# Making weights earlier and summing units later in a fused attention and two-layer feed-forward kernel

## The chip, the cores and the metric

The kernel runs on one core of a Trainium2 chip. Its time is device microseconds of one execution. The engines are TensorE (PE, with its weight loads as PEld), VectorE (DVE), ScalarE (ACT), GpSimd (POOL) and SyncE (SP), which here issues every DMA. Each takes its instructions in the order of its own list.

## The reference

```python
scores = scale * np.matmul(q, k.transpose(0, 1, 3, 2))        # 4 batches, 12 heads, 448 tokens, 64
scores = np.einsum('bhij,hg->bgij', scores, w_pre)
attn = np.exp(scores - np.max(scores, axis=-1, keepdims=True))
attn = attn / (np.sum(attn, axis=-1, keepdims=True) + 1e-09)
attn = np.einsum('bhij,hg->bgij', attn, w_post)
x = np.matmul(attn, v)                                        # as [1792, 768]
h = x @ w_in                                                  # layer 0: w_in [768, 2048]
x = (h * np.cos(h)) @ w_out                                   #          w_out [2048, 768]
g, val = x @ w_gate, x @ w_val                                # layer 1: [768, 1536] each
out = (g * (1.0 / (1.0 + np.exp(-g))) * val) @ w_out2         #          [1536, 768]
```

## The kernel before

Attention comes first. Its 180 blocks are numbered, and each small function (`qk`, `premix`, `post`, `pv_out` and so on) is entered in a plan at the number of a block plus a lag; within one number the tuple `order` sets which kind is issued first. The output of batch b goes by DMA (`pv_out`, L300) to a tile `xs[b]` in memory, and the feed-forward reads it back as token block t = b. `early_plan` enters the first feed-forward work in the same plan, counted from `s`, the first block of the last chunk: the first two column slices of `w_in`, token blocks 0 and 1, and the first layer-0 products of both blocks.

The feed-forward keeps everything as two parts, high and low. A product is three matmuls: high x high, high x low, low x high. The weights come as 64-bit words. A half slab (`w_dma`, 384 KB, a ring of 8 raw buffers) is turned into 32-bit values by `w_shift` on ScalarE and `w_bits`, three VectorE operations (tile `f`), and `w_split` puts the high part on ScalarE and the low part on GpSimd. Slabs of the first product (`i`: w_in, w_gate, w_val) also need their largest absolute value: `w_max` takes it from each half, `w_sum` folds it, `w_sum_all` spreads it over the partitions with a tiny matmul (tile `su`), and `w_unit` makes the scale from that. `w_by` multiplies a slab's scale with the tokens' scale, one number for each token block.

`steps` runs over i. The list `seq` holds (layer, group, token block): 8 groups of 256 columns in layer 0, 6 in layer 1, four blocks each. Step i issues the first product of seq[i] (`l1`, tile `ph`, for both halves e of the group, with `hidden` behind each) and then the second product of seq[i - 1] (`l2`, tile `py`, six pieces m of three banks, each added into `acc`). In layer 0 `hidden` is k, r, Sin, r and the split into `gh` (ScalarE) and `gl` (GpSimd); in layer 1 it is Silu and one product.

The weight work stands in one list, `todo`, that `w_steps` makes: per group 4 pieces for the maxima, 12 for w_out of the group before, 12 for the group's own slabs. `fill(n)` issues up to n pieces where it is called between the matmuls; a piece has a `room`, the step from which it may be issued, and the pieces go strictly in order. `need` issues pieces until a named slab is there. `sum_up`, behind both halves of `l1`, issues `w_sum_all` and `w_unit` of the maxima that are complete.

Between the layers, `next_unit` reduces the six maxima of a finished block of `acc` (tile `mx`), spreads them with a matmul (tile `sx`) and makes the tokens' scale; `next_x` makes the new tokens, two ScalarE operations and one on GpSimd for each of six pieces. `t_new` is the block for which that is due in step i.

Of the kernel before, what the change touches and what calls it, by code (L numbers as in the profile page):

```python
# [7 lines left out]
F32 = mybir.dt.float32  # L8
# [11 lines left out]
B, H, S, D = 4, 12, 448, 64  # L20
# [9 lines left out]
RAWS = 8  # L30
# [7 lines left out]
def attention(ctx, tc, qT, kT, vN, mix, xs, ff):  # L38
# [268 lines left out]
    plan = {}  # L307
# [55 lines left out]
    for i, fn, *a in ff.early_plan(first[B - 1, 3]):  # L363
        at(i, fn, *a)

    order = ("at_hi","l1_part","post","spread","dma_v","w_sum","w_sum_all","w_unit","w_bits","hidden","den","rowmax","rec","norm_hi","dma_k","x_dma","w_dma","new_scale","pv_out","at_lo","norm_lo","lo_k","dma_q","max_v","w_max","w_shift","lo_q","split_v","x_lo","premix","scale_v","w_split","expo","x_hi","qk","hi_k","hi_q","pv")


    with tc.manual_schedule():
# [51 lines left out]
class FeedForward:  # L421


    def __init__(self, ctx, tc, xs, w_in, w_out, w_gate, w_val, w_out2, outT):
        self.ctx, self.tc, self.xs, self.outT = ctx, tc, xs, outT
        self.X, self.raw, self.part, self.G, self.W, self.PH = {}, {}, {}, {}, {}, {}
        self.n_ps = self.n_wi = 0
        self.p_x = self.pool("m_x", 2)
        self.p_const = self.pool("m_const", 1)
        self.ones = self.p_const.tile([128, 128], BF16, name="ones16")  # L430
        self.p_unit = self.pool("m_unit", 4)

        self.unit = [self.p_const.tile([128, 4], F32, name=f"unit{layer}") for layer in range(2)]
        self.scale, self.by = {}, {}
        cols = [w.rearrange("(k p) n -> p k n", p=128) for w in (w_in, w_gate, w_val)]
        rows = [w.rearrange("(f p) (m n) -> f p m n", p=128, n=128) for w in (w_out, w_out2)]
        self.win = [[cols[0]], cols[1:]]
        self.wout = rows
# [88 lines left out]
    def w_shift(self, key, z):  # L527


        nc = self.tc.nc  # L530
        top = self.raw[key, z].bitcast(F32).rearrange("p m (n w) -> p m n w", w=2)[:, :, :, 1]
        t = self.p_wr.tile([128, 3, 128], F32, tag="f", bufs=2, name="f_" + self.nm(key, z))
        by = self.one(key, 4) if key[1] == "i" else 2.0 ** -112
        nc.scalar.activation(t, top, AF.Copy, scale=by)
        self.part[key, z] = t
# [21 lines left out]
    def w_split(self, key, z):  # L557
        nc = self.tc.nc
        first = key[1] == "i"
        tag = self.slab(key)[1]  # L560
        if z == 0:
            pool = self.p_wo if not first else self.p_wi[int(self.n_wi % WI > 1)]
            self.n_wi += first
            self.W[key] = tuple(
                pool.tile([128, 6, 128], F16 if first else F32R, tag=tag + p, name=p + "_" + self.nm(key, z))
                for p in "hl"
            )
            if first and (key[0] == 0 or key[3] > 1):
                self.w_by(key)
        hi, lo = (w[:, 3 * z:3 * z + 3] for w in self.W[key])  # L570
        t = self.part.pop((key, z))
        nc.scalar.copy(hi, t)  # L572
        nc.gpsimd.tensor_tensor(lo, t, hi if first else f(hi), op=ALU.subtract)  # L573
# [25 lines left out]
    def w_steps(self):  # L599


        halves = lambda keys: [(key, z) for key in keys for z in range(2)]
        groups = [(L, g) for L in range(2) for g in range((FF1, FF2)[L] // 256)]
        outs = lambda L, g: [((L, "o", 2 * g + e), z) for z in range(2) for e in range(2)]
        seq = [("conv", outs(0, 0), 0, ("o", 0, 0))]
        for n in range(1, len(groups) + 1):
            for bi, batch in enumerate(self.batches(*groups[n]) if n < len(groups) else [()]):
                room = 4 * (n - 1)
                if batch:
                    seq.append(("max", batch, room, None))  # L610
                if bi == 0 and n > 1:
                    seq.append(("conv", outs(*groups[n - 1]), 4 * (n - 2) + 1, ("o", *groups[n - 1])))
                if batch:
                    seq.append(("conv", halves(batch), room, ("i", *groups[n], bi)))
        self.to_load = []
        out = []
        for kind, what, room, name in seq:
            if kind == "max":
                hs = halves(what)
                for j, (key, z) in enumerate(hs):  # L620
                    out.append((room, None, [
                        *([(self.new_scale, what)] if j == 0 else []), (self.w_max, key, z),
                        *([(self.w_sum, what), (self.sums.append, what)] if j == 3 else []),
                    ]))
                continue
            self.to_load += what
            for j, (key, z) in enumerate(what):
                nxt = what[j + 1] if j + 1 < len(what) else None
                for k in range(3):
                    do = [(self.w_shift, key, z)] if j == k == 0 else []  # L630
                    do.append((self.w_bits, key, z, (k,)))
                    if k == 1 and nxt:
                        do.append((self.w_shift, *nxt))
                    if k == 2:
                        do += [(self.w_split, key, z), (self.load_next,)]
                    out.append((room, name if nxt is None and k == 2 else None, do, key))
        return out
# [76 lines left out]
    def hidden(self, layer, g, t, e, fill=0):  # L714
# [8 lines left out]
        if layer == 0:  # L723
            ps = self.PH[e, 0]
            by, turn = (self.by[0, "i", 0, 2 * g + e][:, i, t:t + 1] for i in range(2))
            k = self.p_t.tile([128, S], I32, tag="t", name=f"k_{g}_{t}_{e}")
            nc.vector.tensor_scalar(k, ps, turn, 0.25, op0=ALU.mult, op1=ALU.add)
            nc.vector.scalar_tensor_tensor(r, ps, turn, k, op0=ALU.mult, op1=ALU.subtract)
            nc.scalar.activation(r, r, AF.Sin, bias=self.hpi, scale=TWOPI)
            self.fill(fill)  # L730
            nc.vector.scalar_tensor_tensor(r, ps, by, r, op0=ALU.mult, op1=ALU.mult)  # L731
        else:
            if g == 0:
                for col in range(2):
                    self.w_by((1, "i", col, e), t)
            by = [self.by[1, "i", col, 2 * g + e][:, 0, t:t + 1] for col in range(2)]
            nc.scalar.activation(r, self.PH[e, 0], AF.Silu, scale=by[0])
            nc.vector.scalar_tensor_tensor(r, self.PH[e, 1], by[1], r, op0=ALU.mult, op1=ALU.mult)  # L738
# [46 lines left out]
    def next_x(self, t, m):  # L785
        nc = self.tc.nc
        hi, lo = (x[:, m] for x in self.X[t])
        x = self.p_t.tile([128, S], F32, tag="nx", bufs=2, name=f"nx_{t}_{m}")
        nc.scalar.activation(x, self.acc[t][:, m], AF.Copy, scale=self.mx[t][:, 7:8])
        nc.scalar.copy(hi, x)  # L790
        nc.gpsimd.tensor_tensor(lo, x, hi, op=ALU.subtract)

    def early_plan(self, s):

        plan = []
        wi = (0, 0, 0, 0), (3, 4, 6, 8)
        x = ((0, 0, 0, 3, 4, 5), (1, 2, 3, 5, 6, 7)), ((6, 7, 8, 9, 10, 11), (8, 9, 10, 11, 12, 13))
        l1 = (6, 7, 7, 9, 9, 9, 9, 11, 11, 12, 12, 12), (14, 15, 16, 16, 16, 16, 17, 17, 17, 17, 20, 22)
# [25 lines left out]

    def steps(self):
        seq = [(L, g, t) for L in range(2) for g in range((FF1, FF2)[L] // 256) for t in range(4)]
        self.sums, self.done, self.mx = [], set(), {}
        self.todo = self.w_steps()
        for _ in range(RAWS):
            self.load_next()  # L830
        done = seq.index((0, 7, 0))
        for t in (2, 3):
            for m in range(6):
                self.x_dma(t, m)
                self.x_hi(t, m)
                self.x_lo(t, m)
                if t == 2:
                    self.now = 0
                    self.fill(2)
        for i in range(1, len(seq) + 1):  # L840
            self.now = i
            t_new = i - done - 2
            if i > 1 and i < len(seq):
# [4 lines left out]
                for e in range(2):  # L848
                    self.l1(L, g, t, e)
                    self.hidden(L, g, t, e, 1)  # L850
                    if e == 0:
                        if 0 <= t_new < 4:
                            self.next_unit(t_new)
                            for m in range(6):
                                self.next_x(t_new, m)
                        self.fill((1, 5)[L])
                self.sum_up()
            L, g, t = seq[i - 1]
            if t == 0:
                self.need(("o", L, g))  # L860
            for m in range(6):
                self.l2(L, g, t, m)
                if m in (1, 3):
                    self.fill(1)
            del self.G[g, t]
# [72 lines left out]
```

## Time and profile before

| | us |
|---|---|
| median of 3 runs | 1581.67 |
| lowest and highest run | 1570.64, 1582.27 |
| the profiled execution | 1579.19 |
| its span, first to last instruction | 1577.4 |
| TensorE busy in it | 1443.9 |
| mean granted TensorE clock | 0.969 |

The profiled execution's own time is 1.8 us above its span and 2.5 us under the median. Attention takes about the first 530 us, layer 0 goes to about 1050, layer 1 to the end. A busy TensorE is not TensorE at its full clock: the granted clock is given as a share of 2.4 GHz.

### The profile page before, as it was taken

The page shows a single profiled execution, that of the slowest core. Times are in us where ns is not written, and L with a number is a line of the kernel's source. Part 1 is how long each engine was busy: PE and PEld are TensorE (multiplying, and loading weights), DVE is VectorE, ACT ScalarE, POOL GpSimd, SP SyncE. Part 2 cuts the span into 40 slices and gives each one's busy share as a digit, 9 for nine tenths or more (in the row PEclk, how much of TensorE's full clock was granted, in tenths as well). Part 3 has the DMA queues.
Part 4 walks back from the last instruction along what each step waited for, and adds up shares of the span by engine and source line. Part 5 has one row for each costly group of instructions (what it writes and reads, how often), then busy time and mean ns, then how long its engine had stood idle before and what let it go on. Part 6 is the DMA issues. An engine that isn't in the chain of part 4 may idle for free.

```text
span 1577.4 us, 27033 instructions
## 1 busy us (share of the span) xinstructions
PE 1443.9 (92%) x10330; PEld 952.4 (60%) x10330; DVE 1067.9 (68%) x2251; ACT 674.2 (43%) x1422; POOL 647.9 (41%) x555
## 2 busy tenths in 40 slices
PE   4899999899997599999999999767999999999999
PEld 2466566565554366666666666445666666666666
DVE  3888888888888557777777787766345656555623
ACT  3677776776765444232232232544342222222210
POOL 1777776776757423232232232434222222222300
PEclk9899999999998799999999999879999999999999
DMA  5454454455453312121121121112121111112002
GB/s 173 127 151 146 142 153 142 141 147 154 140 169 118 117 41 60 32 69 51 36 75 40 41 70 40 51 50 62 49 61 52 53 57 55 47 59 61 1 35 105
DMA packets 93569, 133.06 MB, mean 84 GB/s; under 512 B 18848, under 2 KB 80768, under 8 KB 93440
## 3 DMA queue, kind: packets, MB, share of 16 engines
q1 hardware_dynamic: 93440, 131.34, 28.2%
q8 instruction: 81, 1.33, 0.3%
q14 instruction: 48, 0.39, 0.1%
HBM read 81.59 MB, written 11.01 MB: 59 GB/s over the span
## 4 chain that ended last, share of the span: by engine, by line
PE 68%; DVE 13%; DMA 6%; ACT 6%; issue 3%; POOL 2%; SPq 0%; ACTq 0%; DVEq 0%; POOLq 0%
PE ph L710 10%; PE ph L711 10%; PE ph L712 10%; PE py L755 7%; PE py L757 7%; PE py L756 7%; PE psm L208 6%; DMA x<-s 4%; PE pss L192 3%; PE psv L290 3%; PE psa L257 2%; PE psa L258 1%; PE psa L259 1%; DVE sm L213 1%; DVE r L731 1%
## 5 line engine op out<-in xcount | busy, mean ns | idle before, releaser
L712 PE MATMUL ph<-x,l_i 128*128 128x448 f16 x960 | 340.9, 355 | 4.2 <-POOL l_i L573 4.2
L710 PE MATMUL ph<-x,h_i 128*128 128x448 f16 x960 | 342.2, 356 | 0.0
L711 PE MATMUL ph<-x,h_i 128*128 128x448 f16 x960 | 341.4, 356 | 0.0
L740 POOL TENSOR_TENSOR gl<-r,gh 128x448 fp32r<-128x448 f32 x112 | 135.2, 1207 | 439.0 <-ACT gh L739 428.3
L237 POOL TENSOR_SCALAR eh<-e,sm 120x448 f16<-120x448 f32 x180 | 247.1, 1373 | 139.6 <-DVE sm L232 98.7
L755 PE MATMUL py<-gh,h_o 128*128 128x448 f32 x672 | 262.7, 391 | 42.0 <-ACT acc L759 18.4
L757 PE MATMUL py<-gh,l_o 128*128 128x448 f32 x672 | 252.1, 375 | 2.1 <-POOL l_o L573 1.5
L756 PE MATMUL py<-gl,h_o 128*128 128x448 f32 x672 | 251.5, 374 | 0.0
L761 DVE TENSOR_TENSOR acc<-py,acc 128x448 f32<-128x448 f32 x288 | 174.9, 620 | 81.9 <-PE py L757 79.5
L208 PE MATMUL psm<-x,wpre_sb 120*120 120x448 f32 x360 | 182.5, 590 | 14.7 <-ACT e L221 14.6
L755 PEld LDWEIGHTS py<-gh,h_o 128*128 128x128 f32 x672 | 129.9, 193 | 74.3 <-DVE acc L761 23.4
L710 PEld LDWEIGHTS <-h_i 128*128 128x128 f16 x960 | 94.5, 98 | 116.6 <-issue 25.4
L573 POOL TENSOR_TENSOR l_i<-f_i,h_i 128x384 f16<-128x384 f32 x80 | 80.6, 1009 | 202.3 <-ACT h_i L572 202.3
L257 PE MATMUL psa<-wpost,eh 120*112 120x120 f16 x720 | 133.8, 228 | 19.7 <-DVE at L278 17.9
L712 PEld LDWEIGHTS <-l_i 128*128 128x128 f16 x960 | 94.7, 99 | 94.5 <-POOL l_i L573 5.1
L711 PEld LDWEIGHTS <-h_i 128*128 128x128 f16 x960 | 94.7, 99 | 83.7 <-issue 3.1
L221 ACT ACTIVATE e<-psm,sm 120x448 f32<-120x448 f32 x180 | 115.1, 640 | 62.7 <-DVE sm L232 54.1
L757 PEld LDWEIGHTS py<-gh,l_o 128*128 128x128 f32 x672 | 129.8, 193 | 17.2 <-POOL l_o L573 5.7
L756 PEld LDWEIGHTS py<-gl,h_o 128*128 128x128 f32 x672 | 130.1, 194 | 10.2
L738 DVE SCALAR_TENSOR_TENSOR r<-ph,by_i,r 128x448 f32<-128x448 f32 x48 | 32.8, 684 | 152.3 <-PE ph L712 121.2
L739 ACT CAST gh<-r 128x448 fp32r<-128x448 f32 x112 | 63.4, 566 | 164.5 <-DVE r L738 127.3
L203 ACT COPY s<-pss 120x448 f32<-120x448 f32 (+2 forms) x192 | 96.8, 536 | 85.2 <-DMA x<-s 32.5
(102 smaller groups left out, 2522.9 us busy)
## 6 DMA issues: line engine op xcount, KB each, us to landing
r_o<-in_w_out SPq DMA_DIRECT2D x56, 384.0 KB
x<-s SPq DMA_DIRECT2D x96, 210.0 KB
r_i<-in_w_in SPq DMA_DIRECT2D x32, 384.0 KB
x<-s SPq DMA_DIRECT2D x48, 192.5 KB
r_i<-in_w_gate SPq DMA_DIRECT2D x24, 384.0 KB
r_i<-in_w_val SPq DMA_DIRECT2D x24, 384.0 KB
x<-s SPq DMA_DIRECT2D x48, 175.0 KB
qr<-in_qT SPq DMA_DIRECT2D x15, 360.0 KB
```

Source lines behind the costliest of these rows:

```text
L208: nc.tensor.matmul(ps[:120, :S], wpre_sb, X[b, c][:120, k], start=True, stop=True)
L221: nc.scalar.activation(e, PM.pop((b, c, k))[:120, :S], AF.Exp, bias=sm[:, 0:1], scale=1.0, accum_out=sm[:, 1:2])
L237: nc.gpsimd.tensor_scalar(eh, E[b, c, k], sm[:, 3:4], 1.0, op0=ALU.mult, op1=ALU.mult)
L257: nc.tensor.matmul(o, eh[:, j], wpost_sb[0], start=True, stop=False)
L710: nc.tensor.matmul(ps, wh, xh, start=(kk == 0), stop=False)
L711: nc.tensor.matmul(ps, wh, xl, start=False, stop=False)
L712: nc.tensor.matmul(ps, wl, xh, start=False, stop=(kk == 5))
L740: nc.gpsimd.tensor_tensor(gl, r, f(gh), op=ALU.subtract)
L755: nc.tensor.matmul(ps, wh, gh[:, e], start=(e == 0), stop=False)
L756: nc.tensor.matmul(ps, wh, gl[:, e], start=False, stop=False)
L757: nc.tensor.matmul(ps, wl, gh[:, e], start=False, stop=(e == 1))
L761: nc.vector.tensor_tensor(acc, ps, acc, op=ALU.add)
```

## The change

`early_plan` also enters the first eight loads of the list `todo`, the first four halves of w_out (shift and bits), and loads and splits of token block 2; `load_next` gets a place in `order`. `steps` then only splits those four halves and drops their twelve pieces from the list. `room` falls by eight steps for groups 1 to 7. `next_unit` stands behind both halves of `l1` and behind `sum_up`; `next_x` stands behind each piece of `l2`. Groups 0 and 1 of layer 1 make their `by` for each token block apart. Tile `f` gets four buffers, and `nx` moves to another pool.

```diff
-        t = self.p_wr.tile([128, 3, 128], F32, tag="f", bufs=2, name="f_" + self.nm(key, z))
+        t = self.p_wr.tile([128, 3, 128], F32, tag="f", bufs=4, name="f_" + self.nm(key, z))
...
-            if first and (key[0] == 0 or key[3] > 1):
+            if first and (key[0] == 0 or key[3] > 3):
                 self.w_by(key)
...
-                room = 4 * (n - 1)
+
+                room = 4 * (n - 3) if n < 8 else 24 if n == 8 else 4 * (n - 1)
                 if batch:
                     seq.append(("max", batch, room, None))
...
-            if g == 0:
+            if g < 2:
                 for col in range(2):
-                    self.w_by((1, "i", col, e), t)
+                    self.w_by((1, "i", col, 2 * g + e), t)
...
-        x = self.p_t.tile([128, S], F32, tag="nx", bufs=2, name=f"nx_{t}_{m}")
+        x = self.p_acc.tile([128, S], F32, tag="nx", bufs=2, name=f"nx_{t}_{m}")
...
         plan = []
+        self.todo = self.w_steps()
+        plan += [(s + 10 + j, self.load_next) for j in range(RAWS)]
+        for j in range(4):
+            key = (0, "o", j % 2), j // 2
+            plan.append((s + 18 + j, self.w_shift, *key))
+            plan.append((s + 19 + j, self.w_bits, *key))
+        for m in range(6):
+            plan.append((s + 14 + m, self.x_dma, 2, m))
+            for d, step in enumerate((self.x_hi, self.x_lo)):
+                plan.append((s + 18 + m + d, step, 2, m))
...
-        self.todo = self.w_steps()
-        for _ in range(RAWS):
-            self.load_next()
-        done = seq.index((0, 7, 0))
-        for t in (2, 3):
-            for m in range(6):
-                self.x_dma(t, m)
-                self.x_hi(t, m)
-                self.x_lo(t, m)
-                if t == 2:
-                    self.now = 0
-                    self.fill(2)
+        done = seq.index((0, 7, 0))
+        for j in range(4):
+            self.w_split((0, "o", j % 2), j // 2)
+            self.load_next()
+        self.todo = self.todo[12:]
+        self.done.add(("o", 0, 0))
+        for m in range(6):
+            self.x_dma(3, m)
+            self.x_hi(3, m)
+            self.x_lo(3, m)
...
                     if e == 0:
-                        if 0 <= t_new < 4:
-                            self.next_unit(t_new)
-                            for m in range(6):
-                                self.next_x(t_new, m)
                         self.fill((1, 5)[L])
                 self.sum_up()
+                if 0 <= t_new < 4:
+                    self.next_unit(t_new)
...
             for m in range(6):
                 self.l2(L, g, t, m)
+                if 0 <= t_new < 4:
+                    self.next_x(t_new, m)
                 if m in (1, 3):
                     self.fill(1)
```

ScalarE's list at the end of attention, before. `x_12` is the tile of token blocks 1 and 2, `xr_t_m` a loaded piece of block t, `at0_b_c_k` an attention block, `r0_g_t_e` and `gh0_g_t` the hidden values of layer 0, `f_0_o_f_z` a half of w_out in work.

```order
L691 CAST x_12_9040<-xr_1_3_9102 128x448
L270 ACTIVATE at0_3_3_8895<-psa_3_3_6_9182 112x480
L691 CAST x_12_9040<-xr_2_0_9619 128x448
L729 ACT_TABLE_LOAD
L729 ACTIVATE r0_0_0_0_9256<-r0_0_0_0_9256,hpi_8594 128x448
L534 ACTIVATE f_0_o_0_0_9623<-r_0_o_0_0_9603 128x384
L534 ACTIVATE f_0_o_1_0_9627<-r_0_o_1_0_9605 128x384
L739 CAST gh0_0_0_9254<-r0_0_0_0_9256 128x448
```

The same place, changed.

```order
L693 CAST x_12_9040<-xr_1_3_9102 128x448
L270 ACTIVATE at0_3_3_8895<-psa_3_3_6_9184 112x480
L731 ACT_TABLE_LOAD
L731 ACTIVATE r0_0_0_0_9260<-r0_0_0_0_9260,hpi_8594 128x448
L741 CAST gh0_0_0_9258<-r0_0_0_0_9260 128x448
L693 CAST x_12_9040<-xr_1_4_9157 128x448
L270 ACTIVATE at0_3_3_8895<-psa_3_3_7_9245 112x480
L693 CAST x_12_9040<-xr_1_5_9201 128x448
```

The first piece of block 2 and the first w_out halves have left their places around the first Sin.

VectorE's list in layer 0 before, at the maxima of group 3 (`u_0_i_0_6`): they lie in step (2, 0), behind k and r of half e 0 (`k_2_0_0`). Half e 1 is `k_2_0_1`, and `su` is the result of the spreading matmul.

```order
L727 TENSOR_SCALAR k_2_0_0_10563<-ph0_2_0_0_0_10541,by_0_i_0_4_0_10292 128x448
L728 SCALAR_TENSOR_TENSOR r0_2_0_0_10562<-ph0_2_0_0_0_10541,by_0_i_0_4_0_10292,k_2_0_0_10563 128x448
L495 TENSOR_REDUCE u_0_i_0_6_0_10537<-r_0_i_0_7_1_10431 128x1
L504 TENSOR_TENSOR u_0_i_0_6_0_10537<-u_0_i_0_6_0_10537 128x2
L505 TENSOR_SCALAR u_0_i_0_6_0_10537<-u_0_i_0_6_0_10537 128x2
L506 TENSOR_SCALAR u_0_i_0_6_0_10537<-u_0_i_0_6_0_10537 128x2
...
L542 TENSOR_SCALAR f_0_o_4_0_10574<-f_0_o_4_0_10574 128x384
L727 TENSOR_SCALAR k_2_0_1_10597<-ph0_2_0_1_0_10577,by_0_i_0_5_0_10387 128x448
...
L522 TENSOR_SCALAR u_0_i_0_6_0_10537<-su_0_i_0_6_0_10607 128x2
```

The same maxima, changed: now in step (1, 3).

```order
L729 TENSOR_SCALAR k_1_3_1_10486<-ph0_1_3_1_0_10466,by_0_i_0_3_0_9977 128x448
L730 SCALAR_TENSOR_TENSOR r0_1_3_1_10485<-ph0_1_3_1_0_10466,by_0_i_0_3_0_9977,k_1_3_1_10486 128x448
L496 TENSOR_REDUCE u_0_i_0_6_0_10433<-r_0_i_0_7_1_10431 128x1
L505 TENSOR_TENSOR u_0_i_0_6_0_10433<-u_0_i_0_6_0_10433 128x2
L506 TENSOR_SCALAR u_0_i_0_6_0_10433<-u_0_i_0_6_0_10433 128x2
L507 TENSOR_SCALAR u_0_i_0_6_0_10433<-u_0_i_0_6_0_10433 128x2
L733 SCALAR_TENSOR_TENSOR r0_1_3_1_10485<-ph0_1_3_1_0_10466,by_0_i_0_3_0_9977,r0_1_3_1_10485 128x448
L523 TENSOR_SCALAR u_0_i_0_6_0_10433<-su_0_i_0_6_0_10497 128x2
```

The sum has moved one step ahead, and from the first half of a step into the second; TensorE's matmul `su` stands between the step's last ph and its first py in both. The sums of groups 4 to 7 and the two of layer 1's first group have moved too: of these seven, in steps (1, 3) to (7, 0), four stand like this one and three ahead of their step's first k.

TensorE's list at the first sx, before: between the halves of ph of step (7, 2).

```order
L712 MATMUL ph0_7_2_0_0_13391<-x_12_9040,l_0_i_0_14_0_12861 128x448
L779 LDWEIGHTS ones16_67
L779 MATMUL sx_0_13426<-mx_0_13327,ones16_67 128x1
L710 LDWEIGHTS h_0_i_0_15_0_12955
L710 MATMUL ph0_7_2_1_0_13457<-x_12_9040,h_0_i_0_15_0_12955 128x448
```

The same, changed.

```order
L714 MATMUL ph0_7_2_1_0_13495<-x_12_9040,l_0_i_0_15_0_12676 128x448
L781 LDWEIGHTS ones16_67
L781 MATMUL sx_0_13523<-mx_0_13405,ones16_67 128x1
L757 MATMUL py0_7_1_0_13529<-gh0_7_1_13351,h_0_o_14_0_12839 128x448
```

The matmul sx now stands behind both halves and right ahead of the py run.

## Rows read from the trace of the kernel before

**Rows 1.** The page, the clock in 40 equal slices of the span, tenths.

```profile
PEclk9899999999998799999999999879999999999999
```

**Rows 2.** Waits of TensorE, whole span: us in total, times, longest.

```profile
PE sx L779 <- DVE mx L777: 20.0, 4, 10.0
PE py L755 <- ACT acc L759: 18.4, 5, 11.9
...
PE py L755 <- ACT h_o L572: 8.9, 9, 1.2
...
PE su_i L514 <- DVE u_i L506: 3.5, 1, 3.5
```

**Rows 3.** Windows at run borders: us, busy and instructions by engine, clock, DMA share, GB/s.

```profile
657.50:667.00 9.50, 7.70 (x38) 6.59 (x36) 8.05 (x14) 3.75 (x7) 3.32 (x3) 1.00 0.14 37
673.70:682.70 9.00, 7.96 (x38) 6.54 (x36) 7.84 (x14) 3.78 (x7) 4.69 (x4) 1.00 0.30 87
689.40:697.20 7.80, 7.79 (x38) 6.55 (x36) 7.49 (x14) 2.70 (x5) 3.66 (x4) 1.00 0.26 77
779.50:790.60 11.10, 9.31 (x39) 7.92 (x37) 7.92 (x14) 3.76 (x7) 3.31 (x3) 0.85 0.12 35
682.70:697.20 14.50, 14.49 (x73) 10.05 (x72) 12.43 (x24) 5.08 (x9) 5.41 (x5) 1.00 0.24 71
990.40:1103.90 113.50, 82.48 (x368) 52.76 (x368) 75.57 (x155) 55.57 (x98) 49.06 (x46) 0.86 0.18 53
1125.00:1146.00 21.00, 21.00 (x110) 13.73 (x110) 8.95 (x21) 8.37 (x16) 6.29 (x6) 1.00 0.22 66
530.50:558.20 27.70, 13.36 (x37) 10.18 (x38) 10.97 (x19) 11.01 (x22) 10.80 (x10) 0.63 0.30 93
```

**Rows 4.** Timeline of ScalarE: start, us, instruction, idle before and what ended it.

```profile
531.27 0.41 ACT L299 ACTIVATE xo<-psv 128x300 f32<-128x300 f32 x1
...
551.53 1.40 ACT L759 COPY acc<-py 128x448 f32<-128x448 f32 x3
```

**Rows 5.** The chain of waits, then SP's timeline, at the last loads of x.

```profile
536.82 3.33 DMA xr<-xs
...
542.95 5.79 SPq L685 DMA_DIRECT2D xr<-xs  x6
```

**Rows 6.** ScalarE ahead of the first Sin, and the window just behind that wait.

```profile
510.25 0.56 ACT L691 CAST x<-xr 128x448 f16<-128x448 f32 x1 [4.85 <-DMA xr<-xs]
...
510.00:520.00 10.00, 5.87 (x55) 4.46 (x55) 7.17 (x12) 7.29 (x13) 4.03 (x3) 0.66 0.08 23
```

**Rows 7.** Timeline of VectorE, the bits of one half of w_out.

```profile
534.03 1.15 DVE L542 TENSOR_SCALAR f_o<-f_o 128x384 int32<-128x384 int32 x1
535.21 0.56 DVE L544 SCALAR_TENSOR_TENSOR f_o<-r_o,f_o 128x384 int32<-128x384 int32 x1
535.80 0.56 DVE L548 SCALAR_TENSOR_TENSOR f_o<-r_o,f_o 128x384 int32<-128x384 int32 x1
```

**Rows 8.** Timeline of VectorE, the sum that TensorE's su waited for.

```profile
1027.67 0.16 DVE L504 TENSOR_TENSOR u_i<-u_i 128x2 f32<-128x2 f32 x1
1027.87 0.99 DVE L505 TENSOR_SCALAR u_i<-u_i 128x2 f32<-128x2 f32 x1
```

**Rows 9.** Timeline of TensorE, three of the four sx.

```profile
997.68 0.16 PE L779 MATMUL sx<-mx,ones 128*128 128x1 bf16 x1 [3.66 <-DVE mx L777]
...
1019.44 0.16 PE L779 MATMUL sx<-mx,ones 128*128 128x1 bf16 x1 [3.90 <-DVE mx L777]
...
1084.00 0.16 PE L779 MATMUL sx<-mx,ones 128*128 128x1 bf16 x1 [2.45 <-DVE mx L777]
```

**Rows 10.** Timeline of VectorE ahead of the second sx, from k on.

```profile
1016.51 0.68 DVE L727 TENSOR_SCALAR k<-ph,by_i 128x448 int32<-128x448 f32 x1
...
1018.64 0.68 DVE L731 SCALAR_TENSOR_TENSOR r<-ph,by_i,r 128x448 f32<-128x448 f32 x1 [0.28 <-ACT r L729]
1019.24 0.15 DVE L777 TENSOR_REDUCE mx<-mx 128x1 f32<-128x6 f32 x1
```

More of the change, by code (lines that the diff above doesn't have):

```diff
@@ L364, in attention @@
         at(i, fn, *a)
-    order = ("at_hi","l1_part","post","spread","dma_v","w_sum","w_sum_all","w_unit","w_bits","hidden","den","rowmax","rec","norm_hi","dma_k","x_dma","w_dma","new_scale","pv_out","at_lo","norm_lo","lo_k","dma_q","max_v","w_max","w_shift","lo_q","split_v","x_lo","premix","scale_v","w_split","expo","x_hi","qk","hi_k","hi_q","pv")
+    order = ("at_hi","l1_part","post","spread","dma_v","w_sum","w_sum_all","w_unit","w_bits","hidden","den","rowmax","rec","norm_hi","dma_k","x_dma","w_dma","load_next","new_scale","pv_out","at_lo","norm_lo","lo_k","dma_q","max_v","w_max","w_shift","lo_q","split_v","x_lo","premix","scale_v","w_split","expo","x_hi","qk","hi_k","hi_q","pv")
     with tc.manual_schedule():
@@ L434, in __init__ @@
         self.scale, self.by = {}, {}
+        self.sums, self.done, self.mx = [], set(), {}
         cols = [w.rearrange("(k p) n -> p k n", p=128) for w in (w_in, w_gate, w_val)]
@@ L826, in steps @@
         seq = [(L, g, t) for L in range(2) for g in range((FF1, FF2)[L] // 256) for t in range(4)]
-        self.sums, self.done, self.mx = [], set(), {}
-        self.todo = self.w_steps()
-        for _ in range(RAWS):
+        done = seq.index((0, 7, 0))
+        for j in range(4):
+            self.w_split((0, "o", j % 2), j // 2)
             self.load_next()
-        done = seq.index((0, 7, 0))
-        for t in (2, 3):
-            for m in range(6):
-                self.x_dma(t, m)
-                self.x_hi(t, m)
-                self.x_lo(t, m)
-                if t == 2:
-                    self.now = 0
-                    self.fill(2)
+        self.todo = self.todo[12:]
[4 more added lines that the diff above has]
+            self.x_lo(3, m)
         for i in range(1, len(seq) + 1):
```

## The prediction, made blind

> **What bounds the kernel now.** I read the clock row of the page first, then TensorE's waits over the whole span, then windows cut at the borders of its runs, and only then single engines in the bad stretches. The clock falls in two places, a third and two thirds into the span [rows 1]; the waits name the same two places and one smaller thing [rows 2]. Layer 1 in its steady state (108 matmuls in 21.0 us, all of it busy at full clock) has nothing to give [rows 3]. So three stretches can move.
>
> First, the end of attention. The first run of py takes 27.7 us where a run of 36 such matmuls takes 7.8, with 13.4 us busy at a mean clock of 0.63 [rows 3]; 11.9 us of it is one wait for the copy of py into acc [rows 2]. ScalarE does that copy only after the last x of token block 3, at 551.53, 20 us behind the last attention output at 531.27 [rows 4]; SP issued the loads of that x from 542.95 on [rows 5]. Before that, ScalarE stood 4.85 us for a load of x that is not due: order shows it is block 2's, pulled ahead of the first Sin [rows 6].
>
> Second, layer 0. The pattern repeats every 61 us, six times from 643 on. Of four py runs, the one after a sum takes 9.5 us (11.1 in two of the six, at clock 0.85), the one that needs new w_out weights 9.0, the others 7.8 [rows 3]: 4 x 9.5 + 2 x 11.1 + 6 x 9.0 + 11 x 7.8 = 200 us for 23 runs.
>
> Third, the change of layers: 113.5 us from 990.4 to 1103.9, of which TensorE is busy 82.5 at a mean clock of 0.86 [rows 3]. At full clock its matmuls need 216 in ph and 144 in py, 2 x 6.7 + 2 x 13.5 + 4 x 7.5 = 70.4 us (6.7 is the step of 14.5 less its py run; 21.0 is 13.5 for 72 in ph and 7.5 for a py run, split by the same 0.187 us a matmul in ph). The four matmuls sx wait 20.0 us in all [rows 2].
>
> **The change, part by part.** *End of attention.* Block 2's x, the first w_out halves and their loads get places of their own in attention's plan. The Sin of step (0,0), e 0, then waits only for VectorE's r: 4.85 us earlier, and TensorE's next post with it. What this gains is partly eaten: the bits of four w_out halves, three operations each, now stand on VectorE ahead of the second hidden half of block 1, and ScalarE sends the last attention output behind that. One half costs 1.15 + 0.56 + 0.56 = 2.27 us beside GpSimd's work [rows 7]; if the first operation is short, some 1.5 (an estimate). Four make 6 to 9 us, against the 7 us by which TensorE finishes attention earlier (4.85, and some 2 that it lost at a mean clock of 0.66 after the wait: 5.87 us busy x 0.34 [rows 6]). So I let the last attention output leave when it does now, at 531.7 with its 0.41. After it the queues are free of the rest: SP has no w_out load left to wait for, block 2 is done, and only the write, the read (3.3 us for such a load in the chain of waits [rows 5], so 6 for both with their issue, an estimate) and two casts of 0.6 remain. The copy comes at about 540 instead of 551.5: **-11.5 us**. If VectorE's nine operations are all long and the loads queue behind each other, -5; if the output also leaves earlier, -16. The second group's w_out loads now stand on SP ahead of block 3's first loads and wait for the bits; that is inside the 540.
>
> *The queue two steps ahead.* The same 28 pieces of weight work a group (8 fit in a step) are spread over all four steps, where now the last of four has almost none. The w_out halves are ready a step early: the 9.0 run becomes 7.8. VectorE has room: 12.4 of 14.5 us busy in a step with eight pieces [rows 3]. The places of the sums move, though, and by the order they fall in two ways. In three of the seven sums from step (1, 3) on, the sum is done before the first k of its step and nothing waits. In four, the last maximum and the sum stand on VectorE behind k and r of the step's second half, and TensorE's su stands ahead of the py run. That arrangement exists once before: su waits 3.46 us there [rows 2], of which 0.99 us in an operation on two columns whose like just ahead takes 0.16 [rows 8]; without that stretch 2.7. Such a run then costs 2.7 + 7.5 and what the clock takes. For that the nearest rows are 1.6 us (11.1 against 9.5) and 12 us over six waits in the change of layers (82.5 busy against 70.4 needed), 2.0 each [rows 3]. I take 1.1, between none and 2.0: 11.3 us. Sum: 15 x 7.8 + 4 x 8.3 (the three with an early sum, and the last, which also reduces acc; an estimate between 7.8 and 9.0) + 4 x 11.3 = 195.4, **-4.5 us**. Ends: 10.2 a run gives -9, 13.0 (3.46 and 2.0) gives +2.
>
> The rows: the clock fell in two of the six long runs, and in the stretch of the sx waits of 3.66 and 3.90 us [rows 3, 9]. The Trainium skill, TensorE: Matmul & The Clock Gate, section HAM oscillation, says in my words that gaps between bursts put the array back on its slow clock, so that every burst starts cold. By that rule each of the eight waits of this sum would pay 2.0 us, 16 in place of the 9.4 that I count, and the result would be 6.6 us longer, 1544; its far end is the second rival below.
>
> *Change of layers.* next_unit goes behind both halves of ph, next_x into the py loop, so its 12 ScalarE operations a block lie beside py and the next ph instead of ahead of the Sin. The weights of layer 1's first group are made by then, and w_by for group 1 costs 12 more tiny VectorE operations in steps where TensorE is the bound: nothing, and without that cover some 2 us. sx now waits behind the second half: from the start of k to sx 2.93 us now [rows 9, 10], so 3.1 with the start of k, twice in layer 0; in layer 1 only r and a reduce are left (0.68 + 0.15 [rows 10]), 1.1 us against the 2.45 of now [rows 9], twice. Sum: ph 2 x 6.7 + 2 x 13.5 = 40.4, py 4 x 7.8 = 31.2, waits 8.4, clock 2 x 2.0 + 1 = 5: 85.0 against 113.5, **-28.5 us**. Ends: waits 3.9 and 2.45, clock 8, py at 9.5 give 99, -14; no loss of clock gives -34. Late next would be ScalarE in the first py run of layer 1, where each copy of acc stands behind two operations of next_x; the three banks of ps_y should cover that.
>
> **Sum.** -11.5 - 4.5 - 28.5 = -44.5 on the profiled execution's own 1579.2 us gives 1534.7. The median of the three runs is 2.5 above that execution, so the forecast is 1537.
>
> **The rivals.** *The last block decides.* The wait at the end of attention hangs on the last attention output going out to memory and back, which the change does not move. If the four bits stretch as long as the head start, A is 0: 1549. For it: VectorE and ScalarE are in order, and 9 us of bits against 7. Against it: the loads now issue at 542.95 behind a w_out load.
>
> *The waits that the change makes are paid at half clock.* Su behind the second half four times, sx four times, with the far ends of both terms: +2 and -14, A as above: 1579.2 - 23.5 + 2.5 = 1558. For it: the 0.86 of now; against it: each is followed by a dense run.
>
> *Slower: VectorE becomes layer 0's bound.* Now one step in four is light (two pieces) and drains what is late; afterwards none is. If VectorE needs more than a step's 14.5 us, acc is late in every run, and the 19 ordinary runs cost 11.1 as the worst do now: 19 x 3.3 = 63, against -4.5 - 11.5 - 28.5: 1600. It decides from 2.1 us more VectorE work a step, three operations stretched from 0.35 to 1.15. Against it: the present steps with eight pieces have no wait at 12.4.
>
> *Better than said.* No clock is lost, output earlier: -16 - 9 - 34: 1523.
>
> **How the numbers follow.** Forecast (1526 to 1547) 0.57; last block 0.13; half clock 0.14; better 0.11; VectorE 0.03; the reordering is hidden or lost for a reason that I don't see 0.02. A range of 1519 to 1560 leaves out some 0.15. A measurement of this kernel tells about 1 % from no change: 1566 and 1597. Two of the bad cases together lie near the first bound. So faster 0.90, same 0.07, slower 0.03.
>
> **What would show it.** In the changed profile: no load ahead of the first Sin; the copy of acc 8 to 14 us earlier than 551.5; h_o gone from TensorE's waits in layer 0; four waits of su of 2.7 to 3.5 us there; sx at 3.1, 3.1, 1.1, 1.1; steady layer 1 unchanged at 21.0 a step. I am wrong if the copy does not come earlier, if py runs without a sum pass 8.5 us, or if the stretch between the layers stays above 100.

## The result, and the profile of the changed kernel

| | before | changed |
|---|---|---|
| median of 4 runs, us | 1577.05 | 1536.38 |
| lowest and highest run | 1570.64, 1582.27 | 1532.15, 1538.5 |
| the profiled execution | 1579.19 | 1537.27 |
| its span | 1577.4 | 1535.5 |

The ratio is 0.9741, with a 95% interval of 0.969 to 0.9791. The forecast was 1537.

Of the two dips that the prediction read in the page's clock row [rows 1], the second is gone and the first is left. The page of the changed kernel:

```profile
PEclk9999999999999989999999999999999999999999
```

The waits of TensorE over its whole span (us in total, times, longest), which answer to [rows 2]:

```profile
PE py L757 <- ACT acc L761: 17.1, 4, 14.1
...
PE su_i L515 <- DVE u_i L507: 10.5, 4, 2.6
...
PE sx L781 <- DVE mx L779: 8.2, 4, 3.1
...
PE py L757 <- ACT h_o L573: 2.8, 2, 1.5
...
PE py L757 <- DVE acc L763: 1.0, 5, 0.2
```

The last of these lines was a larger one before, and [rows 2] leaves it out:

```profile
PE py L755 <- DVE acc L761: 14.5, 9, 2.3
```

Sx fell from 20.0 to 8.2 and h_o from 8.9 to 2.8; the waits for VectorE's acc, of which six of 1.8 us stood behind the sums of layer 0, are all but gone; su came, four times 2.63, where before it waited once, in the change of layers. The long wait for ScalarE's acc is still there, and it is longer: 14.1 us against 11.9.

In the windows that follow a step is named by its py run: step (1, 2) is py of group 1, block 2, with the ph ahead of it, which is that of (1, 3). The lists of the change and the prediction go by the ph, and have the same step as (1, 3).

Windows at the borders of runs, with the columns of [rows 3]: the first py run, the steps of two su waits, (1, 2) and (3, 1), the change of layers from the end of py(7, 0) to the end of the first py run of layer 1, and ph and py of step (7, 2) apart.

```profile
523.77:550.35 26.58, 11.67 (x36) 9.32 (x36) 13.90 (x23) 9.65 (x19) 10.43 (x10) 0.68 0.44 126
628.95:646.04 17.09, 14.46 (x75) 10.22 (x74) 12.18 (x26) 3.88 (x7) 3.21 (x3) 1.00 0.11 34
733.23:751.85 18.62, 15.99 (x75) 11.54 (x74) 12.19 (x26) 3.89 (x7) 3.19 (x3) 0.91 0.10 30
978.25:1062.00 83.75, 75.53 (x366) 51.55 (x366) 57.49 (x118) 44.84 (x78) 38.21 (x36) 0.94 0.14 41
997.35:1007.41 10.06, 7.01 (x38) 3.56 (x38) 5.61 (x10) 2.01 (x4) 1.51 (x2) 0.95 0.01 2
1007.41:1017.50 10.09, 10.09 (x37) 8.90 (x37) 6.49 (x14) 8.00 (x14) 7.43 (x7) 0.71 0.00 0
```

So the 41.9 us between the two spans fall into three parts. The end of the first py run comes 7.8 earlier (558.18 to 550.35), almost all of it because that run *starts* 6.7 earlier (530.50 to 523.77); the run itself is 26.6 us where it was 27.7. Layer 0 from there to the end of py(7, 0) takes 427.9 instead of 432.3, 4.4 less. The change of layers takes 83.75 instead of 113.4, 29.7 less. The rest of layer 1 is the same, step by step.

ScalarE at the end of attention, which answers to [rows 4, 6] (start, us, instruction, idle before and what ended it):

```profile
507.01 0.67 ACT L731 ACTIVATE r<-r,hpi 128x448 f32<-128x448 f32 x1 [0.61 <-DVE r L730]
...
530.11 0.51 ACT L573 CAST h_o<-f_o 128x384 fp32r<-128x384 f32 x1 [1.65 <-DVE f_o L549]
531.49 0.67 ACT L731 ACTIVATE r<-r,hpi 128x448 f32<-128x448 f32 x1 [0.86 <-DVE r L730]
532.91 0.56 ACT L741 CAST gh<-r 128x448 fp32r<-128x448 f32 x1 [0.75 <-DVE r L733]
533.38 1.03 ACT L693 CAST x<-xr 128x448 f16<-128x448 f32 x2
534.31 0.41 ACT L299 ACTIVATE xo<-psv 128x300 f32<-128x300 f32 x1
...
541.81 1.12 ACT L693 CAST x<-xr 128x448 f16<-128x448 f32 x2 [2.53 <-DMA xr<-xs]
543.47 0.56 ACT L693 CAST x<-xr 128x448 f16<-128x448 f32 x1 [0.54 <-DMA xr<-xs]
543.94 1.40 ACT L761 COPY acc<-py 128x448 f32<-128x448 f32 x3
```

The first Sin, at 507.01, waits 0.61 us for VectorE and for no load. But the last attention output leaves at 534.31, later than before (531.27), behind splits and a Sin that all wait for VectorE, and the copy of py follows 9.6 us behind it at 543.94. VectorE at that place, the third and fourth half of w_out, then k of the second hidden half of block 1:

```profile
525.58 1.15 DVE L543 TENSOR_SCALAR f_o<-f_o 128x384 int32<-128x384 int32 x1
...
528.82 1.26 DVE L549 SCALAR_TENSOR_TENSOR f_o<-r_o,f_o 128x384 int32<-128x384 int32 x1
530.00 0.67 DVE L729 TENSOR_SCALAR k<-ph,by_i 128x448 int32<-128x448 f32 x1
```

### The profile page after: what moved, and what is told of

Same layout as the page of the kernel before. It is cut to its first block, busy times and chain, and to the rows that moved or that the text cites. A ratio compares the mean times of both kernels' runs of the same rounds, so it can differ in the third digit from the quotient of the medians.

```text
span 1535.5 us, 27113 instructions
## 1 busy us (share of the span) xinstructions
PE 1430.5 (93%) x10330; PEld 949.5 (62%) x10330; DVE 1065.0 (69%) x2263; ACT 670.1 (44%) x1422; POOL 645.3 (42%) x555
## 4 chain that ended last, share of the span: by engine, by line
PE 67%; DVE 16%; DMA 7%; ACT 5%; issue 3%; POOL 1%; SPq 0%; ACTq 0%; DVEq 0%; POOLq 0%
PE ph L712 10%; PE ph L714 10%; PE ph L713 10%; PE py L757 8%; PE py L759 7%; PE py L758 7%; PE psm L208 6%; DMA x<-s 5%; PE pss L192 3%; PE psv L290 2%; DVE r L730 2%; PE psa L257 2%; DVE k L729 2%; DVE r L733 2%; ACT r L731 2%
```

## The experiments

Twelve kernels ran. In all of them the same result is computed; only places and times of instructions differ. The medians of the kernel before beside them were 1577 to 1580. A stage is read from each run's trace as from the two above. The four buffers of `f` and the new pool of `nx` ran only together with other parts; what they do alone is not shown.

**Each part alone.** My theory was that the three terms are separate prices. The rivals were that a part needs another.

*First weights and block 2's x in attention's plan alone* (the diff as shown, without `room`, `next_unit`, `next_x` and `w_by`).

> Only the first weights and block 2's x in attention's plan (with four f buffers and nx in the other pool); rooms, next_unit and next_x as in the kernel before. Theory (the three parts add up): the first py run ends some 7.8 us earlier, as in the changed kernel (550.35 against 558.2), py runs with h_o waits of 0.95 and the 113 us between the layers stay as before: about 1569 us. Rival (the head start is given back, because the queue meets its old rooms and TensorE waits for the same weights at the same time): 1577, with a longer wait somewhere in the first eight steps.

Measured: 1568.65, ratio 0.9951 (0.9926 to 0.9975). The first py run ends 9.0 us earlier and is again not shorter (27.45); layer 0 takes 432.1, the change of layers 111.3. The gain is kept to the end.

*The rooms alone.*

```diff
-                room = 4 * (n - 1)
+                room = 4 * (n - 3) if n < 8 else 24 if n == 8 else 4 * (n - 1)
```

> Only the rooms. Theory (parts add up): the waits for h_o from step (1, 3) on go, four su waits of 2.6 us come, 4.4 us less from the end of the first py run to the end of py(7, 0); the first run stays at 27.7 and the stretch between the layers at 113 us: about 1573. Rival 1 (the queue needs the early loads to get ahead): VectorE or the loads bind in the first groups and waits for h_o stay, 1577 to 1590. Rival 2 (part of the 30 us gained between the layers came from the rooms, since the weights of layer 1's first group are made before it): the stretch falls to 100 or less, 1560.

Measured: 1556.46, ratio 0.9857 (0.9821 to 0.9894). Layer 0 is 6.7 us shorter, with four su waits of 2.63; and the change of layers is 97.6 instead of 113.4. Rival 2 holds: the rooms are worth 16 us where I had given them nothing.

*next_unit and next_x moved, alone* (with `w_by` for each block apart in two groups).

> Only next_unit behind both halves and next_x in the py loop (with by for each block apart in two groups, and nx in the other pool); rooms and first weights as before. Theory (the move alone does it): the stretch from step (7, 1) to the end of the second py run of layer 1 is about 85 us instead of 113.5, sx waits 3.1, 3.1, 1.1, 1.0, about 1547. Rival (the move needs the rooms, since with the old ones the weights of layer 1's first group are made in the same steps): the waits for weights stay in it and it takes 95 to 100: 1560.

Measured: 1564.46, ratio 0.99 (0.986 to 0.994). The rival holds. The change of layers takes 96.2, as this window shows (to the end of the first py run of layer 1, as above), and most of the difference to 83.75 is one wait of the third sx.

```profile
993.60:1089.77 96.17, 76.75 (x368) 52.39 (x367) 73.11 (x147) 51.46 (x92) 46.11 (x43) 0.91 0.22 62
```

The same kernel's third sx on TensorE:

```profile
1057.80 0.16 PE L779 MATMUL sx<-mx,ones 128*128 128x1 bf16 x1 [9.19 <-DVE mx L777]
```

VectorE ahead of it: bits and maxima of layer 1's slabs, one of the maxima waiting for its load, then (left out below) bits of w_out and r of two hidden halves, and the reduction that sx wanted only at the end:

```profile
1036.98 0.35 DVE L542 TENSOR_SCALAR f_i<-f_i 128x384 int32<-128x384 int32 x1
...
1042.84 1.15 DVE L548 SCALAR_TENSOR_TENSOR f_i<-r_i,f_i 128x384 int32<-128x384 int32 x1
1043.91 1.46 DVE L495 TENSOR_REDUCE u_i<-r_i 128x1 f32<-128x384 f32 x3
1047.24 0.55 DVE L495 TENSOR_REDUCE u_i<-r_i 128x1 f32<-128x384 f32 x1 [1.86 <-DMA r_i<-in_w_val]
...
1057.60 0.15 DVE L777 TENSOR_REDUCE mx<-mx 128x1 f32<-128x6 f32 x1
```

The kernel before has the same wait, behind the same weight work. It is the longest of its four sx waits, half of their 20.0 us, and the one that [rows 9] leaves out:

```profile
1056.21 0.16 PE L779 MATMUL sx<-mx,ones 128*128 128x1 bf16 x1 [9.98 <-DVE mx L777]
```

**Which room it is.** The changed kernel with one side of the new rooms taken back.

```diff
-                room = 4 * (n - 3) if n < 8 else 24 if n == 8 else 4 * (n - 1)
+                room = 4 * (n - 3) if n < 8 else 4 * (n - 1)
```

> The changed kernel with the old room, step 28, for layer 1's first group alone. Theory (c_only kept a wait of 9.2 us at the third sx because VectorE makes layer 1's first group in the steps of the change of layers; the room of this group is what takes it out): layer 0 as in the changed kernel, that wait comes back, the stretch from step (7, 1) on takes about 97 us and not 85: 1548. Rival (the lead that the other groups have is enough, since the queue has eight pieces a step): 1536.

Measured: 1551.42, ratio 0.9835 (0.9793 to 0.9876). Layer 0 is much as in the changed kernel (429.1), the change of layers 95.5, with 9.2 us at the third sx again:

```profile
PE sx L781 <- DVE mx L779: 14.8, 4, 9.2
```

```diff
-                room = 4 * (n - 3) if n < 8 else 24 if n == 8 else 4 * (n - 1)
+                room = 24 if n == 8 else 4 * (n - 1)
```

> The changed kernel with the old rooms for groups 1 to 7 and step 24 for layer 1's first group. Theory (the step 24 is worth something only when the queue is ahead by then; with the old rooms group 7 itself is made from 24 on): the wait at the third sx is back as in c_only, and layer 0 has its h_o waits again and no su waits: 1550. Rival (one early room is all that the change of layers needs): layer 0 as before, the stretch at 85 to 88, 1541.

Measured: 1553.48, ratio 0.9843 (0.9811 to 0.9875). Change of layers 92.9, the third sx waits 8.6, the h_o waits are back (8.9 us over the whole span), and of the su waits one of 2.63 is left in layer 0, where I had expected none. So step 24 is worth its 12 us only with the lead of the groups before it; without that lead the stretch is 3.3 us under c_only's.

**The waits that the change made.** The sum of four su waits and their clock was 14.9 us over four ordinary steps of 14.5.

```diff
-                self.sum_up()
...
-                if m in (1, 3):
+                if m == 2:
+                    self.sum_up()
+                if m in (2, 4):
                     self.fill(1)
```

> The changed kernel with sum_up behind the third piece of the py loop and the two fills of that loop behind the third and fifth piece. Theory (the four long steps of layer 0, 18.6, 18.6, 18.6 and 17.1 us where the others take 14.5, are long for the su wait of 2.63 and for the clock behind it): those steps fall to 14.5 to 15, 14.9 us less: about 1521. Rival (the wait moves: w_unit on VectorE then stands between the adds of acc, and the py run with a sum waits for acc as before's did, 1.8 us in seven steps): 1534.

Measured: 1519.83, ratio 0.9624 (0.9589 to 0.966). Layer 0 takes 411.5, 16.4 less than in the changed kernel, and the wait came back nowhere. Step (1, 2) of this kernel:

```profile
631.84:646.33 14.49, 14.41 (x74) 10.21 (x74) 11.71 (x25) 3.91 (x7) 3.23 (x3) 1.00 0.13 42
```

The four sx waits, in the same way:

```diff
                     if e == 0:
+                        if 0 <= t_new < 4:
+                            self.tc.nc.vector.tensor_reduce(
+                                out=self.mx[t_new][:, 6:7], in_=self.mx[t_new][:, :6], axis=AX.X, op=ALU.max
+                            )
```

and the same reduction taken out of `next_unit`.

> The changed kernel with one move: the reduction of a finished block's six maxima stands on VectorE behind the first half of ph instead of the second; the matmul sx stays. Theory (sx waits 3.1, 3.1, 1.2 and 0.9 us because its reduction is queued behind k and r of the second half, and the clock then takes some 3.6 us in the two runs behind the long waits): all four waits go, -11.8: about 1525. Rival (the clock is low there for another reason than these waits): 8.2 go, 1528. Second rival (sx then waits for the maximum of the last piece, which comes late): unchanged, 1536.

Measured: 1528.49, ratio 0.9687 (0.966 to 0.9714). From the trace the change of layers takes 73.1, 10.6 less; one sx waits 0.9, for `w_unit` ahead of it, and the others wait 0.1 or not at all. The granted clock of the stage is 1.00, so the loss of clock does go with the waits, as the first theory has it:

```profile
979.89:1053.02 73.13, 71.56 (x366) 47.77 (x366) 56.57 (x118) 44.91 (x79) 38.76 (x36) 1.00 0.17 48
```

The size is less sure than the 10.6 looks. The median is 7.9 less, and hid_late below, which has the same four sx waits as the changed kernel, needs 81.1 us for the stage, 7.9 more than here:

```profile
974.53:1055.60 81.07, 72.85 (x366) 49.28 (x366) 57.40 (x118) 44.84 (x78) 38.20 (x36) 0.98 0.15 43
```

The other 2.7 us are clock that the changed kernel's profile lost behind its second sx and hid_late's did not (last section).

**The first py run.** Three tries at the 14.1 us wait. First block 3's casts behind the run:

```diff
         for m in range(6):
-            self.x_dma(3, m)
-            self.x_hi(3, m)
-            self.x_lo(3, m)
+            if m < 4:
+                self.x_dma(3, m)
...
+            for m in range(6) if i == 1 else ():
+                self.x_hi(3, m)
+                self.x_lo(3, m)
+                if m < 2:
+                    self.x_dma(3, m + 4)
             del self.G[g, t]
```

> The changed kernel with the casts and low parts of block 3's x behind the first py run instead of ahead of it (its first four loads stay, two come behind the casts). Theory (the 14.1 us wait in the first py run is the place of the first copy of py on ScalarE, behind six casts that wait for their loads): the copy follows the last attention output, 535 instead of 543.9, and 9 us go: about 1527. Rival (the loads of block 3 are what is late): the wait turns up in ph(0, 3) or later, 1536.

Measured: 1534.81, ratio 0.9726 (0.9702 to 0.9749), not to be told from the changed kernel. The first run is 9.4 us shorter (17.14), as the theory had it; but TensorE pays before and after, and layer 0 takes 435.1, 7.2 us more. TensorE behind it, in step (0, 1): su waits, and py waits for a copy of acc that now stands behind the six casts:

```profile
552.55 0.18 PE L515 MATMUL su_i<-u_i,ones 128*128 128x2 bf16 x1 [1.61 <-DVE u_i L507]
...
559.17 0.47 PE L757 MATMUL py<-gh,h_o 128*128 128x448 f32 x1 [2.66 <-ACT acc L761]
```

And VectorE ahead of it: block 3's low parts no longer stand ahead of the queue's first maximum, and that has moved up between k and r of the hidden values of (0, 0), where it waits for its load. A ph ahead of the run waited 3.3 us for what stands behind it.

```profile
512.70 0.55 DVE L496 TENSOR_REDUCE u_i<-r_i 128x1 f32<-128x384 f32 x1 [2.59 <-DMA r_i<-in_w_in]
```

Then the other end, the output itself: `hid = (12, 14), (19, 22)` becomes `(12, 14), (19, 27)`.

> The changed kernel with hidden of step (0, 1), e 1, five plan numbers later, behind the last attention output. Theory (that output leaves at 534.3 and not at 531.7 as I said, since ScalarE has four splits and a Sin ahead of it that wait for VectorE's twelve bits): it leaves some 3 us earlier, at 531, and the first copy of py with it, 540.5 instead of 543.9: about 1533. Rival (TensorE or the read back sets it): no change, 1536.

Measured: 1529.73, ratio 0.9698 (0.9667 to 0.9728). ScalarE in this kernel:

```profile
528.53 0.42 ACT L299 ACTIVATE xo<-psv 128x300 f32<-128x300 f32 x1
...
539.62 1.12 ACT L693 CAST x<-xr 128x448 f16<-128x448 f32 x2 [3.08 <-DMA xr<-xs]
540.64 1.39 ACT L761 COPY acc<-py 128x448 f32<-128x448 f32 x3
```

The output leaves 5.8 us earlier, more than I expected, and the copy only 3.3, as expected: 12.1 us behind the output instead of 9.6. By the chain of waits the last two loads stand behind GpSimd's low part of an earlier piece, which frees their buffer. So no single place sets the copy; the run is 24.0 instead of 26.6.

Last both, with the casts a run later and the queue's first pieces kept out of attention's tail (the first loop over block 3 keeps only its first four loads, as in x3_late):

```diff
-        hid = (12, 14), (19, 22)
+        hid = (12, 14), (19, 27)
...
-                self.fill((3, 5)[L])
+                self.fill((3, 5)[L] if i > 2 else 0)
...
-                        self.fill((1, 5)[L])
+                        self.fill((1, 5)[L] if i > 2 else 4)
...
-                if m in (1, 3):
-                    self.fill(1)
+                if i == 2:
+                    self.x_hi(3, m)
+                    self.x_lo(3, m)
+                    if m < 2:
+                        self.x_dma(3, m + 4)
+                if i > 1 and m in (1, 3):
+                    self.fill(1 if i > 2 else 2)
```

> The changed kernel with block 3's casts one run later (in the second py run, each behind a copy of acc), hidden of (0, 1), e 1, behind the last attention output, and the queue's first pieces behind k and r of step (0, 2) so that no maximum stands in attention's tail. Theory (the wait of the first py run is the place of ScalarE's copy behind work that waits; block 3's x itself is due only at ph(0, 3)): first run 13 us instead of 26.6, second step 14.8 as now, -13.5: about 1523. Rival (what x3_late showed is the rule: the loads are late wherever the casts stand): the wait comes back in the second or third run, 1533 or more.

Measured: 1526.43, ratio 0.9699 (0.9657 to 0.9741). The first run takes 13.4 and the first two steps 31.3 us instead of 41.4; layer 0 gives 4.9 back, 3.1 of it in step (0, 1), where a sum now stands (su waits 1.9). Three places moved at once here; which of them the gain needs is not shown.

**All together.** With su_late, sx_early and x3_late in one kernel, hidden late, and the third and fourth half of w_out made during the first py run (their bits eight plan numbers later, their splits ahead of its second and third piece):

> The changed kernel with the three moves of the runs before (sum_up behind the third piece of py, the reduction of the maxima behind the first half of ph, block 3's casts behind the first py run), hidden of (0, 1), e 1, behind the last attention output, and the second w_out halves made during the first py run. If the waits of su, of sx and of the first copy are separate prices, the sum is -16.5 - 11.8 - 14 on 1536.4: 1494. If they share the clock's loss, or one shift uncovers another wait, 1505 or more.

Measured: 1513.48, ratio 0.9592 (0.9564 to 0.962). The second case: layer 0 and the change of layers keep their gains, but the first two steps take 40.6 us, nearly what they take in the changed kernel. Py waits 5.5 us for the late h_o and 4.6 for acc. That led to x3b_hid, and with the two other moves to the last kernel:

> x3b_hid with sum_up behind the third piece of py and the reduction of the maxima behind the first half of ph: the three places that cost time in the changed kernel, mended together. From all_five's 1513.5 the first two steps fall from 40.6 to 28: about 1500. If the end of attention gives its gain back again: 1512.

Measured: 1500.78, ratio 0.9526 (0.9487 to 0.9566), 36 us below the changed kernel. Its first py run, its step (1, 2) and its change of layers (the first two steps take 29.8):

```profile
522.26:535.56 13.30, 9.87 (x36) 7.34 (x37) 9.92 (x13) 6.26 (x13) 7.44 (x7) 0.87 0.75 212
619.46:633.96 14.50, 14.43 (x75) 10.22 (x74) 11.72 (x25) 3.90 (x7) 3.23 (x3) 1.00 0.13 42
952.42:1025.10 72.68, 71.50 (x366) 47.57 (x366) 57.90 (x119) 44.75 (x79) 39.47 (x37) 1.00 0.17 48
```

Its waits of TensorE: su is gone from the list, and sx has one wait.

```profile
PE py L757 <- ACT acc L761: 7.2, 5, 2.1
...
PE sx L780 <- DVE mx L860: 0.5, 1, 0.5
```

## Why the prediction was right, point by point

**End of attention: -7.8 where I had -11.5, the term that was off.** That the first Sin loses its wait for a load, and TensorE some 7 us with it, was right (6.7 in this pair; the last section shows how far that start moves by itself). The step that failed is "So I let the last attention output leave when it does now, at 531.7": that is the end of its 0.41 us, and it ended at 534.72. I had set 6 to 9 us of bits against 7 us of head start; the four halves' bits end at about 530, and behind the third and the fourth ScalarE still has two splits, a Sin and the split of gh, each waiting for VectorE. The 8.3 us from there to the copy came out as 9.2. So what this term gained is almost all the head start of TensorE, and the first py run kept its wait; the rival "the last block decides" was half true. hid_late and x3_late show that moving one end gains 3 us or nothing, x3b_hid that nearly all of the wait can go.

**Layer 0: -4.4 against -4.5.** Its parts fit as well. What goes is the waits for VectorE's acc and for h_o, what comes is su and its clock. The four runs with a late sum cost 46.3 us with their waits (I had 45.2), the other 19 cost 149.8 (150.2). The waits are 2.63 each, by the price I had without the long operation on two columns. su_late shows the price as a whole: without these waits layer 0 is 16.4 us shorter. VectorE did not become the bound.

**Change of layers: -29.7 against -28.5, the right size with a wrong owner.** The waits of sx are 3.11, 3.05, 1.16 and 0.90, 8.2 in sum for my 8.4. TensorE is busy 75.5 us where 70.4 are needed, so the clock takes 5.1 for my 5. That fit is luck in part: hid_late, with the same waits, is busy 72.9 us and loses 2.4. But I gave it all to the moved next_unit and next_x. Alone they gain 17.3; about 12 hang on the room of layer 1's first group, as room_28 shows, and on the lead of the groups before it, as room_24 does. I had written that this group's weights "are made by then" without asking which edit does that: it is the 24 in the diff, four steps under the old room, which the description of the change passes over. What I did not look at is the longest of the four sx waits, 9.98 us, which [rows 9] leaves out and the sum lets fall to 1.1: it stood behind just this weight work, and moving next_unit alone left 9.19 of it in place. The two parts overlap: alone they gain 17.3 and 15.9, in the whole change 29.7.

**The sum** of the profiled pair is -41.9 for my -44.5: the first term is 3.7 short and the third 1.2 over. That the median came out only 0.6 below the forecast is luck. The 2.5 us that I put between the profiled execution and the median came from three runs; with the fourth, the median of the kernel before lies 2.1 below that execution, and the changed kernel's lies 0.9 below its own. This error and the short sum cancel.

**The rival of half clock.** I had counted 1.1 us of clock behind an su wait, between none and 2.0. In the changed kernel three of the four py runs behind su took 8.98 and one 7.45, which is 1.1 on average, though no single run lost 1.1. The clock granted tells them apart [the windows above: 0.91 in step (3, 1), 1.00 in step (1, 2)]. Not every wait pays, and this rival's 1558 was far off. So was the 1544 that the prediction worked out with all eight waits paying 2.0 us: five paid, three behind su and two behind sx, and the clock took some 9.5 us behind all eight, close to the 9.4 counted. The Trainium skill, TensorE: Matmul & The Clock Gate, section HAM oscillation, describes cold bursts behind waits for a DMA, longer than most of these, so the 1544 asks more of that page than it states.

## What to carry to other kernels

When an edit moves several things, run each alone before the sum is believed: here a right total hid that 12 of the 29.7 us of one term belonged to another edit. A queue of background work that is made to run ahead pays where it empties an engine's list in a later bad stretch, not only where its own waits were. And a copy that TensorE needs should stand ahead of work that waits for loads, in the engine's own list; moving it behind other waiting work only moved the wait (x3_late), and it went where three places of the chain were moved together (x3b_hid).

## What was not expected of the hardware

The loss of clock behind one and the same wait is not one price: it can be nothing, and where it comes, its size differs. Three of TensorE's waits in the changed kernel, in time:

```profile
638.56 0.16 PE L515 MATMUL su_i<-u_i,ones 128*128 128x2 bf16 x1 [2.63 <-DVE u_i L507]
...
988.35 0.16 PE L781 MATMUL sx<-mx,ones 128*128 128x1 bf16 x1 [3.11 <-DVE mx L779]
...
1007.38 0.16 PE L781 MATMUL sx<-mx,ones 128*128 128x1 bf16 x1 [3.05 <-DVE mx L779]
```

Eight kernels have such su waits in layer 0 (a wait of 2.63 us, then 36 matmuls of py), and 28 runs stand behind one: 23 take 8.95 to 9.00 us, four take 7.4, and one, the only one of room_24, takes 10.2 at a granted clock of 0.70:

```profile
942.12 0.16 PE L515 MATMUL su_i<-u_i,ones 128*128 128x2 bf16 x1 [2.63 <-DVE u_i L507]
...
942.15:952.38 10.23, 10.23 (x37) 9.04 (x37) 4.59 (x10) 1.48 (x3) 1.14 (x1) 0.70 0.01 2
```

Behind the second sx, with 3.05 us in five kernels, the run took 10.09 in the changed kernel and 7.40 or 7.41 in the four others. The same ph and the same py run in hid_late, in windows as above:

```profile
993.63:1003.70 10.07, 7.02 (x39) 3.57 (x38) 5.61 (x10) 2.02 (x4) 1.50 (x2) 1.00 0.01 2
1003.70:1011.10 7.40, 7.40 (x38) 6.66 (x37) 6.36 (x14) 6.69 (x12) 5.55 (x6) 1.00 0.00 0
```

Same wait, same matmuls: a granted clock of 0.71 over that run in the one (part of it at 1.2 GHz), 1.00 (2.4 GHz) in the other. In the changed kernel the clock had fallen before that run began (0.95 over 997.35:1007.41, the ph and the wait), in hid_late it had not (1.00). The Trainium skill, TensorE: Matmul & The Clock Gate, section HAM oscillation, tells of a kernel in which every burst behind a wait starts cold. Here that is so for 24 of 28 runs behind su, and behind the second sx for one in five. The measured runs decide: a wait of this length is a chance of the loss, and why a given one pays, and how much, stays open.

The end of attention moves by itself. In the changed kernel, su_late, sx_early, a_only, room_28 and room_24 every engine has the same list up to the first py run, and that run starts at 523.77, 526.18, 525.02, 521.71, 521.70 and 521.17. The kernel before, b_only and c_only share their lists in the same way and start it at 530.50, 532.52 and 533.41. So the head start is 8.9 us between the two means, and the 6.7 of the profiled pair is one draw of it. These 5 us are as large as the smaller terms of this study, and a stage's own length in the trace tells them where a median cannot.
